# The MLP's token mixing done per pair of heads, and the start, the order of steps and the PSUM banks laid out anew

## The chip, the cores and the metric

The kernel runs on one core of one Trainium2 chip. The time is the device time of one execution in microseconds. Three executions of the kernel before gave 315.58, 315.77 and 318.79, so the median is 315.77 us. The engines are TensorE (PE; PEld is its weight load), VectorE (DVE), ScalarE (ACT), GpSimd (POOL) and SyncE (SP), and each works through its own instructions in their program order.

## The reference

Two stages follow each other. The first is causal attention over 4 batches of 8 heads, 768 positions and 64 dimensions, in which each position sees only its own block of 64 keys and the three blocks with the highest gate scores:

```python
k_rep = k.reshape(B, H, n_blocks, 64, D).mean(axis=3)
gate_scores = einsum('bhsd,bhnd->bhsn', q, k_rep)       # future blocks: -1e9
top_idx = argsort(gate_scores)[..., -3:]                # and the own block
scores = where(chosen block and causal, q @ k.T / sqrt(D), -1e9)
x[b, s, 64 h + d] = softmax(scores) @ v
```

The second is a mixer MLP on `x`, which has 768 positions and 512 channels per batch:

```python
u = x + (relu(x.T @ w_tok1) @ w_tok2).T                 # token mixing, 768 -> 256 -> 768
out = u + relu(u @ w_ch1) @ w_ch2                       # channel mixing, 512 -> 1536 -> 512
```

Token mixing runs over the positions, and every channel stands by itself in it. Channel mixing needs all 512 channels of a position.

## The kernel before

The work goes by pairs of heads (16 pairs, four to a batch) and by heads (32). For each pair, `ktr` transposes K in two halves on TensorE (three fp32 transposes each), copies both heads' parts to `KA` and sums each block's keys on VectorE; `ksd` spreads these sums; `qtr` transposes Q in two halves, and ScalarE copies each half to `QT`; `qcast` makes the 16-bit `QA` of it; `gate` multiplies Q with the block sums (five fp32 matmuls) and finds the third largest score of each row with ten maxima on VectorE; `btr` transposes the resulting bias rows, which go into `QA` as extra contraction rows. Against them, `KA` holds an indicator of the key's block. For each head, `scores` then makes three groups of transposed scores in one of two PSUM tiles of two banks (`sc0`, `sc1`), ScalarE takes their exponential into `E`, `dmask` (GpSimd) zeroes the causal corners, and `avmm` multiplies by V with 21 small matmuls; VectorE divides by the row sum and writes the head's 64 columns of `x`.

The MLP of a batch is a list of steps: `tok1` (two times six matmuls with 512 columns, one column for each channel), `umix` (six times two matmuls with 512 columns, then the residual added on VectorE), `utr` (u transposed, copied by ScalarE), `ch1` (24 steps of four matmuls with 384 columns, with a relu that ScalarE and VectorE take in turn) and `ch2` (six steps of 12 matmuls with 512 columns, a residual on VectorE and a store).

Everything else draws PSUM from a ring of four banks (`bank`). For the last batch `all_banks` adds the four halves of `sc0` and `sc1` at the ring's end.

The order on every engine is set by one list of events: `at(t, f, ...)` gives a step a place t in units of one head, the list is sorted by t, and the functions are called in that order. Head n has its scores at n to n + 0.66 and its `avmm` at n + 1.2; a pair p is prepared from 2p - 3.4 to 2p - 1.2; the MLP of batch b stands evenly, by its matmul columns, between 8(b + 1) + 0.45 and 8(b + 2) + 0.4, so that it lies between the heads of the next batch. The prediction calls such a unit a slot. Loads stand in SyncE's queue, weights in GpSimd's, constants in ScalarE's.

Of the kernel before, what the change touches and what calls it, by code (L numbers as in the profile page):

```python
# [45 lines left out]
def kernel(  # L46
# [65 lines left out]
    h1T = sb([128, 2, DM], F16, "h1T")  # L112
# [19 lines left out]
    def all_banks():  # L132
        ring.extend(t[:, 512 * i:512 * i + 512] for t in sc for i in range(2))
# [13 lines left out]
    own1 = np.where(nidx[None, None, :] == mrow, 0.0, -1.0).astype(np.float16)  # L147
# [75 lines left out]
    def gate(p):  # L223
# [12 lines left out]
        for x in range(2):  # L236
            nc.vector.scalar_tensor_tensor(out=bn[r][:, :, 64 - 64 * x:64 - 64 * x + NB],
                                           in0=ge[r][:, :, NB * x:NB * x + NB],
                                           scalar=1.0, in1=own[:, :, NB * x:NB * x + NB],
                                           op0=ALU.subtract, op1=ALU.max)  # L240

    def btr(p):
# [3 lines left out]
        nc.vector.tensor_copy(out=QA[p % RQ][64:64 + NB, 0, 128:S], in_=t[64:64 + NB, :])  # L246
        nc.vector.tensor_copy(out=QA[p % RQ][0:NB, 1, 128:S], in_=t[0:NB, :])
# [41 lines left out]
    def mlp(b):  # L289
        x, u, ut = xb[b % 2], u16[b % 2], uT[b % 2]  # L290
        th = []

        def tok1(t):
            m = bank()
            for j in range(NJ):
                nc.tensor.matmul(out=m, lhsT=w1[:, j, 128 * t:128 * t + 128], rhs=x[:, j, :],  # L296
                                 start=(j == 0), stop=(j == NJ - 1))
            nc.scalar.activation(out=h1T[:, t, :], in_=m, func=AF.Relu)

        def umix(j):  # L300
            m = bank()
            for t in range(2):
                nc.tensor.matmul(out=m, lhsT=w2[:, t, 128 * j:128 * j + 128], rhs=h1T[:, t, :],
                                 start=(t == 0), stop=(t == 1))
            nc.vector.tensor_tensor(out=u[:, j, :], in0=x[:, j, :], in1=m, op=ALU.add)  # L305

        def utr(j):
            t = bank()[:, 0:256].bitcast(F16)
            for c in range(NCC):
                nc.tensor.transpose(out=t[:, 128 * c:128 * c + 128], in_=u[:, j, 128 * c:128 * c + 128], identity=id16)  # L310
            copy(nc.scalar, ut[:, :, 128 * j:128 * j + 128], t.rearrange("p (c s) -> p c s", s=128))

        def ch1(f, i):
            m = bank()[:, 0:HS]
            for c in range(NCC):
                nc.tensor.matmul(out=m, lhsT=wc1[:, c, 128 * f:128 * f + 128],  # L316
# [102 lines left out]
```

## Time and profile before

| what | us |
|---|---|
| median of three executions | 315.77 |
| the profiled execution | 319.9 |
| its span (first to last instruction) | 318.2 |
| PE busy | 276.8 (87%) |
| DVE busy | 176.6 (55%) |
| ACT busy | 148.3 (47%) |
| POOL busy | 89.2 (28%) |

The profiled execution is 4.1 us above the median and 1.7 us longer than its own span. The busy time of TensorE is the time in which a matmul is under way, and matmuls overlap, so a busy engine is not one at its peak; how far a stretch is from that is read by setting the time of its steps in a dense stretch, one after another, against the time that it took.

### The profile page before, as it was taken

The numbers are of one execution on the slowest core, as the hardware profiler recorded it, in microseconds if no ns is written. First come the engines' busy times: TensorE is split into PE (matmuls) and PEld (weight loads), VectorE is DVE, ScalarE is ACT, GpSimd is POOL, SyncE is SP. The second block draws the span as 40 slices with busy tenths as digits, with TensorE's granted clock in tenths as the row PEclk, the third lists the DMA queues.
The fourth block names the chain that finished last, engine by engine and source line by source line (L and its number), as shares of the span: only waits on it lengthen the run. The fifth ranks groups of instructions, "written<-read, shape, count | busy, mean of one in ns | idle before, by whom it ended". The sixth has DMA issues, their size and how long they took to land.

```text
span 318.2 us, 5946 instructions
## 1 busy us (share of the span) xinstructions
PE 276.8 (87%) x2224; PEld 178.0 (56%) x2224; DVE 176.6 (55%) x533; ACT 148.3 (47%) x233; POOL 89.2 (28%) x167
## 2 busy tenths in 40 slices
PE   2678787698999999889999999889999996778994
PEld 2566575555767665546676656556775453444441
DVE  5966966648575746556757455486755222433221
ACT  1126754657666434556756434466664341532100
POOL 2426756631314141413232333214141120000000
PEclk9999977969999999989999999799999999999999
DMA  8999999995200015896200019800000120000022
GB/s 171 220 218 214 155 215 206 204 230 103 68 21 0 20 50 142 201 222 116 51 2 0 35 66 212 186 0 4 2 0 13 55 98 36 0 1 2 33 81 84
DMA packets 82492, 29.73 MB, mean 93 GB/s; under 512 B 76168, under 2 KB 78880, under 8 KB 82464
## 3 DMA queue, kind: packets, MB, share of 16 engines
q1 hardware_dynamic: 78464, 25.17, 36.5%
q0 software_dynamic: 3232, 3.93, 7.8%
q10 hardware_dynamic: 768, 0.26, 0.4%
q8 instruction: 17, 0.28, 0.4%
q14 instruction: 11, 0.09, 0.1%
HBM read 27.00 MB, written 6.29 MB: 105 GB/s over the span
## 4 chain that ended last, share of the span: by engine, by line
PE 72%; DVE 15%; ACT 3%; DMA 3%; issue 2%; POOL 2%; SPq 0%; DVEq 0%; ACTq 0%; POOLq 0%
PE pm L316 17%; PE pm L327 16%; PE sc L259 9%; PE pm L279 6%; PE pm L227 6%; PE pm L296 4%; PE sc L327 3%; DVE u L305 3%; DVE KA L91 3%; PE pm L202 3%; PE sc L316 2%; PE pm L216 2%; DMA wc<-in_moe_w_ch_dram 2%; DVE ks L205 2%; DMA k<-in_k_dram 1%
## 5 line engine op out<-in xcount | busy, mean ns | idle before, releaser
L262 ACT ACTIVATE E<-sc 128x1024 f16<-128x1024 f32 (+1 forms) x96 | 87.6, 918 | 77.0 <-PE sc L259 72.1
L270 POOL TENSOR_SCALAR_AFFINE_SELECT E<-E 128x256 f16<-128x256 f16 x96 | 39.3, 409 | 158.0 <-ACT E L262 157.0
L316 PE MATMUL pm<-uT,wc 128*128 128x384 f16 x336 | 64.4, 326 | 0.0
L259 PE MATMUL sc<-QA,KA 76*128 76x512 f16 (+7 forms) x256 | 55.7, 325 | 0.0
L327 PE MATMUL pm<-wc,h 128*128 128x512 f16 x240 | 54.9, 379 | 0.0
L316 PEld LDWEIGHTS <-wc 128*128 128x128 f16 x384 | 36.2, 98 | 24.3 <-issue 5.0
L327 PEld LDWEIGHTS <-h 128*128 128x128 f16 x288 | 27.5, 98 | 32.4 <-issue 2.1
L259 PEld LDWEIGHTS <-KA 76*128 76x128 f16 (+1 forms) x256 | 25.4, 107 | 16.9 <-issue 2.2
L322 DVE TENSOR_SCALAR h<-pm 128x384 f16<-128x384 f32 x42 | 23.3, 555 | 18.8 <-PE pm L316 18.5
L331 DVE TENSOR_TENSOR osb<-u,pm 128x512 f32<-128x512 f16 x20 | 13.8, 688 | 35.4 <-PE pm L327 29.9
L279 PE MATMUL pm<-VA,E 128*128 128x65 f16 x672 | 29.2, 200 | 3.4 <-POOL E L270 2.5
L279 PEld LDWEIGHTS <-E 128*128 128x128 f16 x672 | 27.7, 102 | 6.5 <-POOL E L270 4.3
L227 PE MATMUL pm<-ks,QT 128*128 128x24 f32 x160 | 22.4, 283 | 9.7 <-DVE ks L211 9.3
L227 PEld LDWEIGHTS pm<-ks,QT 128*128 128x128 f32 x160 | 22.2, 213 | 12.6 <-ACT E L262 6.8
L205 DVE TENSOR_REDUCE ks<-pm 128x6 f32<-128x384 f32 x32 | 17.4, 544 | 19.5 <-ACT KA L89 19.5
L320 ACT ACTIVATE h<-pm 128x384 f16<-128x384 f32 x42 | 20.5, 489 | 14.5 <-PE pm L316 14.4
L91 POOL CAST QA<-QT 64x768 f16<-64x768 f32 x30 | 24.7, 822 | 9.2 <-ACT QT L217 7.3
L91 DVE CAST KA<-pm 64x384 f16<-64x384 f32 x40 | 22.3, 557 | 2.8 <-PE pm L202 2.1
L202 PE MATMUL pm<-id,k 128*128 128x128 f32 x96 | 19.1, 318 | 5.4 <-DMA k<-in_k_dram 5.4
L217 ACT COPY QT<-pm 128x384 f32<-128x384 f32 x32 | 15.4, 480 | 15.4 <-PE pm L216 15.4
L202 PEld LDWEIGHTS pm<-id,k 128*128 128x128 f32 x96 | 14.0, 171 | 8.7 <-issue 7.3
L285 DVE TENSOR_TENSOR x<-pm,rc 128x384 f16<-128x384 f32 x32 | 17.8, 557 | 1.1
(50 smaller groups left out, 266.6 us busy)
## 6 DMA issues: line engine op xcount, KB each, us to landing
k<-in_k_dram SPq DMA_DIRECT2D x32, 192.0 KB, 4.3
q<-in_q_dram SPq DMA_DIRECT2D x32, 192.0 KB, 4.5
v<-in_v_dram SPq DMA_DIRECT2D x16, 384.0 KB, 5.3
out_dram<-osb SPq DMA_DIRECT2D x24, 256.0 KB, 2.0
wc<-in_moe_w_ch_dram POOLq DMA_DIRECT2D x8, 384.0 KB, 6.7
w<-in_moe_w_tok_dram POOLq DMA_DIRECT2D x2, 384.0 KB, 6.6
id<-id32c ACTq DMA_DIRECT2D x1, 64.0 KB
gbias<-gbiasc ACTq DMA_DIRECT2D x1, 60.0 KB, 3.1
```

The lines of the kernel that those rows point to most:

```text
L91: e.tensor_copy(out=out, in_=in_)
L202: nc.tensor.transpose(out=t[:, 128 * j:128 * j + 128], in_=k32[p % RL][:, 3 * i + j].rearrange("p x d -> p (x d)"), identity=id32)
L205: nc.vector.tensor_reduce(out=ks[p % 2][:, 6 * i:6 * i + 6], in_=t.rearrange("p (n w) -> p n w", w=64), axis=mybir.AxisListType.X, op=ALU.add)
L227: nc.tensor.matmul(out=o[:, j, :], lhsT=QT[r][:, 128 * (j + 1):128 * (j + 2)], rhs=ks2[r].rearrange("p x n -> p (x n)"), start=True, stop= ...
L259: nc.tensor.matmul(out=t[:, at:at + 128 * m], lhsT=KP[0:K, x, 128 * kk:128 * kk + 128], rhs=QP[0:K, x, 128 * q0:128 * (q0 + m)], start=Tru ...
L262: nc.scalar.activation(out=E[n % RE][:, 1024 * g:1024 * g + WIDTH[g]], in_=t[:, 0:WIDTH[g]], func=AF.Exp, scale=scale)
L270: nc.gpsimd.affine_select(out=o, in_=o, pattern=[[0, 2], [1, 128]], compare_op=ALU.is_ge, fill=0.0, base=0, channel_multiplier=-1)
L279: nc.tensor.matmul(out=t[:, jq, :], lhsT=e[:, c:c + 128], rhs=va[:, x, kk, :], start=(kk == 0), stop=(kk == jq))
L316: nc.tensor.matmul(out=m, lhsT=wc1[:, c, 128 * f:128 * f + 128], rhs=ut[:, c, HS * i:HS * i + HS], start=(c == 0), stop=(c == NCC - 1))
L320: nc.scalar.activation(out=o, in_=m, func=AF.Relu)
L322: nc.vector.tensor_scalar(out=o, in0=m, scalar1=0.0, scalar2=None, op0=ALU.max)
L327: nc.tensor.matmul(out=m, lhsT=h2[:, f, 128 * j:128 * j + 128], rhs=wc2[:, f, :], start=(f == 0), stop=(f == NFC - 1))
```

## The change

Token mixing is done per pair of heads. `tok1(p)` takes the pair's 128 channels of `x` (two times six matmuls with 128 columns into one bank, one relu of 256 columns), `umix(p, i)` makes three blocks of positions for these channels in one bank (six matmuls with 128 columns) with one residual of 384 columns, and `utr(p)` transposes the pair's six blocks, with one copy of 768 columns, on VectorE where ScalarE did it before. Only `ch1` and `ch2` are left in the list of the batch; batch b's list starts at 8(b + 1) + `CH[b]` and ends shortly ahead of the next.

At the start, the identity is loaded first, the two gate constants are one tensor (without the copy for the second head), the unused triangle is not loaded, the 16-bit identity is a VectorE cast, the block indicators come by DMA straight into `KA` instead of by six GpSimd copies, and V of pair 0 is loaded behind K and Q of pair 1. K's sums stand ahead of its copies, which ScalarE makes wholly for the first five pairs and by half later. The places of all steps of a pair come from tables by phase (`LEAD`, `MIX`). `all_banks` puts the halves of `sc0` and `sc1` between the four banks, in turn.

```diff
 def all_banks():
-    ring.extend(t[:, 512 * i:512 * i + 512] for t in sc for i in range(2))
+    halves = [t[:, 512 * i:512 * i + 512] for i in range(2) for t in sc]
+    first = [ring[(rn[0] + i) % 4] for i in range(4)]
+    ring[:] = [t for two in zip(first, halves) for t in two]
+    rn[0] = 0
...
+id32 = const(np.eye(128, dtype=np.float32), "id32", nc.scalar)
 load(k32, k, 0, nc.sync)
 load(q32, q, 0, nc.sync)
-id32 = const(...); gbias = const(...); own = const(...); id16 = const(...); m0 = const(...)
-nc.scalar.dma_start(out=ind[0:NB, :], in_=indc)
-nc.scalar.dma_start(out=ind[64:64 + NB, :], in_=indc)
-load(v32, v, 0, nc.sync)
+gown = const(np.ascontiguousarray(np.stack([gb1, own1], axis=1)[:, :, 1:]), "gown", nc.scalar)
+def indicators(r, eng):
+    eng.dma_start(out=KA[r][64:64 + NB, 0, :], in_=indc)
+    eng.dma_start(out=KA[r][0:NB, 1, :], in_=indc)
+nc.vector.memset(KA[0][0:64, 1, :], 0.0)
+indicators(0, nc.scalar)
 load(k32, k, 1, nc.sync)
 load(q32, q, 1, nc.sync)
+load(v32, v, 0, nc.sync)
...
 def ktr(...):
-    copy(e0, KP[0:64, 0, c], t[0:64, :])
     nc.vector.tensor_reduce(out=ks[p % 2][:, 6 * i:6 * i + 6], ...)
-    copy(e1, KP[64:128, 1, c], t[64:128, :])
+    copy(e[0], KP[0:64, 0, c], t[0:64, :])
+    copy(e[1], KP[64:128, 1, c], t[64:128, :])
...
+def tok1(p):
+    b, c = divmod(p, NCC)
+    m = bank()[:, 0:256]
+    for t in range(2):
+        for j in range(NJ):
+            nc.tensor.matmul(out=m[:, 128 * t:128 * t + 128], lhsT=w1[:, j, 128 * t:128 * t + 128],
+                             rhs=xb[b % 2][:, j, 128 * c:128 * c + 128], start=(j == 0), stop=(j == NJ - 1))
+    nc.scalar.activation(out=h1T[p % 2].rearrange("p t c -> p (t c)"), in_=m, func=AF.Relu)
+def umix(p, i):
+    m = bank()[:, 0:HS]
+    for j in range(3):
+        for t in range(2):
+            nc.tensor.matmul(out=m[:, 128 * j:128 * j + 128],
+                             lhsT=w2[:, t, 128 * (3 * i + j):128 * (3 * i + j) + 128],
+                             rhs=h1T[p % 2][:, t, :], start=(t == 0), stop=(t == 1))
+    nc.vector.tensor_tensor(out=u16[b % 2][o], in0=xb[b % 2][o], in1=m.rearrange(...), op=ALU.add)
+def utr(p, e):
+    t = bank()[:, 0:HS].bitcast(F16)
+    for j in range(NJ):
+        nc.tensor.transpose(out=t[:, 128 * j:128 * j + 128], in_=u16[b % 2][:, j, 128 * c:128 * c + 128], identity=id16)
+    copy(e, uT[b % 2][:, c, :], t)
...
+LEAD = [
+    dict(k0=-1.82, k1=-2.59, q0=-1.73, q1=-1.31, ks=-1.1, qc=-0.88, gt=-0.84, vc=-0.16, bt=-0.18),
...
+    dict(k0=-2.32, k1=-1.92, q0=-3.08, q1=-2.09, ks=-1.66, qc=-0.95, gt=-1.43, vc=0.18, bt=-0.52),
+]
+MIX = {2: dict(t1=2.61, u0=3.03, u1=3.03, ut=3.42), 3: dict(t1=2.5, u0=3.05, u1=3.16, ut=3.4)}
+KE = [(A, A), (A, A), (A, A), (V, A)]
+AV, MASK = (1.25, 1.18), 0.23
+CH = [1.69, 1.91, 1.71, 1.9, 0.66]
...
+    at(t0 + o["t1"], tok1, p)
+    at(t0 + o["u0"], umix, p, 0)
+    at(t0 + o["u1"], umix, p, 1)
+    at(t0 + o["ut"], utr, p, V)
...
-    t0, t1 = H * (b + 1) + 0.45, H * (b + 2) + 0.4
+    t0, t1 = H * (b + 1) + CH[b], H * (b + 2) + CH[b + 1] - 0.05
```

Three places of the order are shown, each before and then with the change. In the rows a number behind a name is that of a buffer, and xN counts instructions alike.

The first is VectorE at the start, from the first K transposes (`pm_117`, `pm_118`) to the gate of pair 0 (`gm_87`). Before:

```order
L91 CAST KA_75<-pm_117 64x384
L205 TENSOR_REDUCE ks_83<-pm_117 128x6
...
L91 CAST KA_75<-pm_118 64x384
L205 TENSOR_REDUCE ks_83<-pm_118 128x6
...
L211 COPY ks_0_85<-ks_83 64x12 x2
L91 CAST QA_72<-QT_81 64x768 x2
L229 TENSOR_TENSOR gm_87<-pm_117,gbias 128x120
```

With the change:

```order
L178 CAST id_138<-id_122 128x128
L207 TENSOR_REDUCE ks_83<-pm_118 128x6
L207 TENSOR_REDUCE ks_83<-pm_119 128x6
L214 COPY ks_0_85<-ks_83 64x12 x2
L91 CAST QA_72<-QT_81 64x768 x2
L235 TENSOR_TENSOR gm_87<-pm_118,gown 128x120
```

The four casts into `KA` have left VectorE's queue; they stand in ScalarE's, ahead of the copies to `QT`.

The second is TensorE behind the gate of pair 0, up to the first scores (`sc`). Before, K's and Q's transposes of pair 1 and its gate (`ks_1_86`) stand ahead of them:

```order
L227 MATMUL pm_117<-ks_0_85,QT_81 128x24 x5
L202 MATMUL pm_118<-id_125,k_1_67 128x128 x3
L245 LDWEIGHTS bn_93
...
L202 MATMUL pm_120<-id_125,k_1_67 128x128 x3
L216 MATMUL pm_117<-id_125,q_1_64 128x128 x3
L216 MATMUL pm_118<-id_125,q_1_64 128x128 x3
L227 MATMUL pm_119<-ks_1_86,QT_82 128x24 x5
L259 LDWEIGHTS KA_75
L259 MATMUL sc_115<-QA_72,KA_75 128x512
```

With the change:

```order
L231 MATMUL pm_118<-ks_0_85,QT_81 128x24 x5
L219 MATMUL pm_119<-id_122,q_1_64 128x128 x3
L251 LDWEIGHTS bn_93
...
L219 MATMUL pm_121<-id_122,q_1_64 128x128 x3
L265 LDWEIGHTS KA_75
L265 MATMUL sc_116<-QA_72,KA_75 128x512
```

K's transposes and the gate of pair 1 now stand between and behind the first scores; only Q's transposes are left ahead of them.

The third is ScalarE in batch 0, from the first exponential of one pair of heads to that of the next. Before:

```order
L262 ACTIVATE E_97<-sc_115 128x1024
L262 ACTIVATE E_97<-sc_116 128x1024
L262 ACTIVATE E_97<-sc_115 128x640
L262 ACTIVATE E_95<-sc_116 128x1024
L217 COPY QT_82<-pm_119 128x384
L262 ACTIVATE E_95<-sc_115 128x1024
L217 COPY QT_82<-pm_117 128x384
L262 ACTIVATE E_95<-sc_116 128x640
```

With the change:

```order
L268 ACTIVATE E_97<-sc_116 128x1024
L89 CAST KA_77<-pm_120 64x384 x2
L221 COPY QT_81<-pm_121 128x384
L89 CAST KA_77<-pm_118 64x384 x2
L268 ACTIVATE E_97<-sc_117 128x1024
L302 ACTIVATE h1T_102<-pm_121 128x256
L268 ACTIVATE E_97<-sc_116 128x640
L268 ACTIVATE E_95<-sc_117 128x1024
L268 ACTIVATE E_95<-sc_116 128x1024
L268 ACTIVATE E_95<-sc_117 128x640
L221 COPY QT_82<-pm_119 128x384
```

The four casts of K and the relu of token mixing have come into the queue, between the first and the third exponential of the pair.

## Rows read from the trace of the kernel before

**Rows 1.** Stages: from:to us, length, then busy us of engines, PEclk, DMA share.

```profile
21.60:66.50 44.90, 35.81 (x347) 27.64 (x347) 32.31 (x122) 26.44 (x37) 27.52 (x49) 0.88 1.13 201
66.50:134.50 68.00, 65.22 (x556) 42.14 (x556) 41.29 (x128) 38.49 (x61) 20.51 (x39) 0.98 0.38 86
134.50:202.70 68.20, 65.34 (x557) 42.31 (x557) 41.29 (x128) 37.47 (x60) 19.45 (x37) 0.98 0.42 94
202.70:265.10 62.40, 59.35 (x501) 36.71 (x501) 31.78 (x86) 32.09 (x50) 14.12 (x29) 0.98 0.13 36
265.10:277.00 11.90, 7.82 (x49) 3.68 (x49) 4.10 (x6) 4.12 (x7) 0.00 (x0) 1.00 0.06 22
277.00:297.00 20.00, 16.53 (x98) 9.35 (x96) 6.13 (x11) 6.47 (x13) 0.00 (x0) 1.00 0.01 1
297.00:318.20 21.20, 15.90 (x73) 6.84 (x70) 4.68 (x7) 0.00 (x0) 0.00 (x0) 1.00 0.20 74
```

**Rows 2.** Chain that ended last, 66 to 110 us: start us, us, what.

```profile
69.87 1.30 PE pm L296 x6
...
76.11 0.22 PE pm L310 x4
...
80.25 0.65 PE pm L316 x4
80.90 1.03 PE pm L227 x10
...
82.58 0.44 PE sc L259 x3
...
83.67 0.66 PE pm L279 x21
...
86.72 0.33 PE pm L202 x3
...
88.62 0.28 PE pm L245 x5
...
106.80 2.59 PE pm L327 x12
```

**Rows 3.** Timeline of the start: start us, us, engine, line, operation, [idle before <-releaser].

```profile
9.08 0.48 ACT L217 COPY QT<-pm 128x384 f32<-128x384 f32 x1 [0.16 <-PE pm L216]
...
10.66 2.30 PE L227 MATMUL pm<-ks,QT 128*128 128x24 f32 x10 [1.62 <-DVE ks L211]
...
15.05 0.69 PE L245 MATMUL pm<-id,bn 128*128 128x128 f16 x5 [1.38 <-DVE bn L237]
...
19.42 2.30 PE L227 MATMUL pm<-ks,QT 128*128 128x24 f32 x10 [1.75 <-DVE ks L211]
...
22.61 1.02 ACT L262 ACTIVATE E<-sc 128x1024 f16<-128x1024 f32 x1 [4.43 <-PE sc L259]
```

**Rows 4.** Timeline of TensorE in batch 0, one gate.

```profile
50.97 1.27 PE L227 MATMUL pm<-ks,QT 128*128 128x24 f32 x10 [1.95 <-DVE ks L211]
```

**Rows 5.** Groups by line and shape: busy us, mean ns, idle before.

```profile
L262 ACT ACTIVATE E<-sc 128x1024 f16<-128x1024 f32 x64 | 65.4, 1024 | 70.7 <-PE sc L259 70.3
...
L262 ACT ACTIVATE E<-sc 128x640 f16<-128x640 f32 x32 | 22.6, 706 | 6.3 <-POOL QA L91 3.6 <-PE sc L259 1.8
...
L217 ACT COPY QT<-pm 128x384 f32<-128x384 f32 x32 | 15.4, 480 | 15.4 <-PE pm L216 15.4
...
L89 ACT CAST KA<-pm 64x384 f16<-64x384 f32 x24 | 11.2, 468 | 6.0 <-PE pm L202 5.8
```

**Rows 6.** Waits from 264 us to the end: us in total, times, longest.

```profile
PE sc L316 <- ACT h L320: 3.5, 6, 0.6
```

**Rows 7.** The last piece of the chain, columns as in rows 2.

```profile
314.50 0.69 DVE osb L331
```

**Rows 8.** Waits of the whole span, columns as in rows 6.

```profile
PE pm L296 <- DVE x L285: 2.6, 2, 1.3
...
PE pm L310 <- DVE u L305: 5.1, 7, 1.2
```

More of the change, by code (lines that the diff above doesn't have):

```diff
@@ L286, in avmm @@
                                 in1=r.broadcast_to([128, NJ, 64]), op=ALU.mult)
[L289 to L294, printed above, removed]
-            for j in range(NJ):
[L296 to L301, printed above, removed]
-            for t in range(2):
[L303 to L316, printed above, removed]
-                                 rhs=ut[:, c, HS * i:HS * i + HS], start=(c == 0), stop=(c == NCC - 1))
-            o = h2[:, f, HS * i:HS * i + HS]
-            if f % 2 == 0:
-                nc.scalar.activation(out=o, in_=m, func=AF.Relu)
-            else:
-                nc.vector.tensor_scalar(out=o, in0=m, scalar1=0.0, scalar2=None, op0=ALU.max)
-        def ch2(j):
-            m = bank()
-            for f in range(NFC):
-                nc.tensor.matmul(out=m, lhsT=h2[:, f, 128 * j:128 * j + 128], rhs=wc2[:, f, :],
-                                 start=(f == 0), stop=(f == NFC - 1))
-            o = osb[osn[0] % 3]
-            osn[0] += 1
-            nc.vector.tensor_tensor(out=o, in0=u[:, j, :], in1=m, op=ALU.add)
-            nc.sync.dma_start(out=out[b, 128 * j:128 * j + 128, :], in_=o)
-        th += [(3072, lambda t=t: tok1(t)) for t in range(2)]
-        for j in range(NJ + 1):
-            if j < NJ:
-                th.append((1024, lambda j=j: umix(j)))
-            if j >= 1:
-                th.append((512, lambda j=j: utr(j - 1)))
-        th += [(1536, lambda f=f, i=i: ch1(f, i)) for i in range(2) for f in range(NFC)]
-        th += [(6144, lambda j=j: ch2(j)) for j in range(NJ)]
-        return th
@@ new lines, in utr, with ch1 @@
+    def utr(p, e):
+        b, c = divmod(p, NCC)
+        t = bank()[:, 0:HS].bitcast(F16)
+        for j in range(NJ):
+            nc.tensor.transpose(out=t[:, 128 * j:128 * j + 128], in_=u16[b % 2][:, j, 128 * c:128 * c + 128],
+                                identity=id16)
+        copy(e, uT[b % 2][:, c, :], t)
+    def ch1(b, f, i):
+        m = bank()[:, 0:HS]
+        for c in range(NCC):
+            nc.tensor.matmul(out=m, lhsT=wc1[:, c, 128 * f:128 * f + 128],
+                             rhs=uT[b % 2][:, c, HS * i:HS * i + HS], start=(c == 0), stop=(c == NCC - 1))
+        o = h2[:, f, HS * i:HS * i + HS]
+        if f % 2 == 0:
+            nc.scalar.activation(out=o, in_=m, func=AF.Relu)
+        else:
+            nc.vector.tensor_scalar(out=o, in0=m, scalar1=0.0, scalar2=None, op0=ALU.max)
@@ new lines, in ch2 @@
+    def ch2(b, j):
+        m = bank()
+        for f in range(NFC):
+            nc.tensor.matmul(out=m, lhsT=h2[:, f, 128 * j:128 * j + 128], rhs=wc2[:, f, :],
+                             start=(f == 0), stop=(f == NFC - 1))
+        o = osb[osn[0] % 3]
+        osn[0] += 1
+        nc.vector.tensor_tensor(out=o, in0=u16[b % 2][:, j, :], in1=m, op=ALU.add)
+        nc.sync.dma_start(out=out[b, 128 * j:128 * j + 128, :], in_=o)
+    A, V, G = nc.scalar, nc.vector, nc.gpsimd
+    LEAD = [
+        dict(k0=-1.82, k1=-2.59, q0=-1.73, q1=-1.31, ks=-1.1, qc=-0.88, gt=-0.84, vc=-0.16, bt=-0.18),
+        dict(k0=-1.95, k1=-1.61, q0=-2.79, q1=-2.08, ks=-1.36, qc=-1.44, gt=-1.26, vc=-0.16, bt=-0.34),
+        dict(k0=-1.76, k1=-1.87, q0=-2.04, q1=-1.83, ks=-1.75, qc=-1.49, gt=-1.6, vc=-0.89, bt=-0.84),
+        dict(k0=-2.32, k1=-1.92, q0=-3.08, q1=-2.09, ks=-1.66, qc=-0.95, gt=-1.43, vc=0.18, bt=-0.52),
+    ]
@@ L374 @@
             at(n + 0.33 * g, scores, n, g)
[L375 to L376 removed]
+            at(n + 0.33 * g + MASK, dmask, n, g)
+        at(n + AV[0 if n < H else 1], avmm, n)
+    at(2 * NP - 0.1, all_banks)
     for b in range(B):
[L378 to L382 removed]
+        th = [(1536, ch1, b, f, i) for i in range(2) for f in range(NFC)] + [(6144, ch2, b, j) for j in range(NJ)]
+        total = sum(c for c, *_ in th)
+        t0, t1 = H * (b + 1) + CH[b], H * (b + 2) + CH[b + 1] - 0.05
         done = 0
[L384 to L385 removed]
+        for c, f, *a in th:
+            at(t0 + (t1 - t0) * done / total, f, *a)
             done += c
```

99 lines of the change are left out of this document (48 added, 51 removed).

## The prediction

> **What bounds the kernel now.** I read the stages first [rows 1], then the chain of waits in the dense part for the price of each step [rows 2], then the start [rows 3], one cycle of batch 0 [rows 4], and the end [rows 6, 7]. From 66.5 us to 265 us TensorE is under way for 95% of each stage, and the chain there is nearly one matmul step after another. So I take the time of a step in that chain as its price at the full clock, add up the whole kernel in these prices, and call what is left of the span the loss. The change can only win out of the loss, or change the work.
>
> Prices in us: three K transposes 0.33, and three for Q, the same instruction on another tensor, as much; a gate 1.03; the five bias transposes 0.28; a score group of 1024 columns 0.44, so one of 640 columns 0.28; an `avmm` 0.66; four `ch1` matmuls 0.65; twelve `ch2` matmuls 2.59; six `tok1` matmuls of 512 columns 1.30; four transposes of u 0.22 [rows 2].
>
> A pair of heads: 0.66 + 0.66 + 1.03 + 0.28 + 2 x (0.44 + 0.44 + 0.28) + 2 x 0.66 = 6.27, of which 2.63 is its preparation; 16 pairs are 100.3. Channel mixing of a batch: 24 x 0.65 + 6 x 2.59 = 31.1; four are 124.6. Token mixing of a batch: 2 x 1.30, as much for the twelve `umix` matmuls of equal width, and 6 x 0.22, so 6.5; four are 26.1. The work is 251.0, and the loss 318.2 - 251.0 = 67.2.
>
> Where it lies, by stage. Up to 66.5 us, slot 8.45, TensorE has done 31.0 of work (five preparations and a sixth without its bias transposes 15.5; scores of eight heads and two groups 10.2; eight `avmm` 5.3): a loss of 35.5. Batches 1 and 2 [rows 1] hold 6.27 x 4 + 6.5 + 31.1 = 62.7 of work in 68.0 and 68.2: 5.3 and 5.5. The stage of 62.4 holds what is left, 57.0: 5.4. After attention, 53.1 for 37.6: 15.5.
>
> **The work added.** `tok1` and `umix` turn 24 matmuls of 512 columns per batch into 96 of 128, each with its own weight load. The nearest row is the u transposes, 128 columns with a load each, at 0.22 / 4 = 0.055 us; `avmm`, 65 columns with a load each, runs at 0.66 / 21 = 0.031 [rows 2], so a load does not set the pace down to there. I take 0.055: a pair's token mixing is 30 x 0.055 = 1.65, in all 26.4 against 26.1. The work becomes 251.3. The bounds are 0.053 (a quarter of the 512-column matmul, 2.59 / 48) and 0.076, the mean time of a weight load in batch 1 (42.14 us over 556, [rows 1]), should nothing of it hide.
>
> The Trainium skill, "TensorE: Matmul & The Clock Gate", section "Back-to-back issue gap", speaks against this part: it gives 81 ns a matmul for a sustained stream of load and matmul at 128 columns, and 131 ns at 512. By it the 384 matmuls would cost 384 x 0.026 = 10.0 us more than in my sum, which would end at 294. The trace disagrees with it at both widths, with 55 ns and 216 ns, and I go by the rows.
>
> **The start, to the first scores.** Now the gate of pair 0 starts at 10.66, 1.1 us after the second half of QT is there (9.08 + 0.48), since VectorE is still making K's casts and sums; and the first scores wait for a second gate, which starts at 19.42, so that the first exponential is at 22.61 [rows 3]. With the casts on ScalarE, ahead of the QT copies but in time that it waited for Q, the sums are spread before QT is copied, so the gate starts at 9.7. It takes the same 2.3 us (low clock: it takes 1.03 at the full one). The bias transposes come 15.05 - 12.96 = 2.1 later and take 0.7, the copies of the bias some 0.7 more: scores at 15.5, the first exponential at 16.4, 6.2 earlier. Fewer constants, the direct indicators and the identity cast save nothing more on this path, which runs through K, Q and the gate; their engines have room there. V of pair 0, behind K and Q of pair 1, is wanted only by the first `avmm`, after that exponential.
>
> **Batch 0.** Its 44.9 us hold 8.45 slots, so 10.6 us for each pair, against 6.27 of work. The row shows why: every gate waits some 1.95 us for VectorE's sums [rows 4], and such a wait is followed by a low clock (mean 0.88 in the stage, [rows 1]). Now token mixing joins, so TensorE has 7.9 per pair. ScalarE has 2 x (2 x 1.024 + 0.706) + 2 x 0.48 + 4 x 0.468 [rows 5] and a relu of 256 columns, under 0.48, say 0.38: 8.7. VectorE's 7.6 (32.31 x 10.6 / 44.9) lose four casts and gain two adds and a copy: about 7. So ScalarE sets the floor. Following its queue from the first exponential of a pair: QT is whole after 1.02 + 2 x 0.47 + 0.48 = 2.4; the gate (1.03), `tok1` (0.66) and the third score group (0.28) then run while ScalarE makes two casts and the second exponential (to 4.4), the relu and the third (to 5.5) and the fourth (to 6.5). The fifth wants scores that stand behind the next `avmm`, which wants the third exponential masked: about 7.3. So it waits 0.7, and the cycle is 8.7 + 0.7 + 0.1 = 9.5. TensorE waits for QT about 0.6 a cycle in place of 1.95, and the clock should hold. Bounds: 8.7, and 10.6 + 1.65 = 12.2, if every wait stays and token mixing is added to it.
>
> Channel mixing now starts at slot 9.69: 15.5 + 4.85 x 9.5, and 1.0 for pair 5's first steps that stand beside pair 4's: 62.6 us. Work done by then: preparations 16.4, ten heads' scores 11.6, nine `avmm` 5.9, four token mixings 6.6: 40.5. The loss is 22.1.
>
> **Batches 1 to 3.** What goes is token mixing as one block: `tok1` waiting for the last head's x, transposes waiting for the adds [rows 8], and the low clock behind it (0.98, [rows 1]). In the new order a pair's `avmm`, `tok1`, `umix` and `utr` stand 0.32, 0.55 and 0.24 slots apart, 2.5, 4.3 and 1.9 us, with `ch1` or `ch2` between. What is late next is VectorE, strictly in order: 41.3 of 68 now, about 44 of 65 with u's copies from ScalarE; adds, a u copy, a relu and a gate's ten maxima come close together, and each holds one of four banks. I take a loss of 2.5 a batch, half of today's; the bounds are 0.7 and today's 5.4. Three: 7.5.
>
> **The end.** The last pair's steps stand between three `ch2` steps of batch 2; exposed are about a relu (0.6) and a u copy (0.9). In `ch1`, 20.0 us for 15.6 of work, TensorE waits six times for a relu where both halves of one `sc` tile stand next to each other in the ring [rows 6]; with the halves four places apart I leave 0.5 for this and for `ch2`. From the last residual to the end 3.7 stay [rows 7]. Together 5.7, against 15.5.
>
> **The sum.** 251.3 + 22.1 + 7.5 + 5.7 = 286.6, that is 31.6 less than the span, so 288.3 for the profiled execution's 319.9. The median is 4.1 below that one; taking 31.6 from 315.77 gives 284.
>
> **The rivals.** (a) *Batch 0 keeps its waits*: a cycle of 12.2 adds 4.85 x 2.7 = 13, so 297; halfway it is 291. For it: ScalarE is loaded to nine tenths, and all queues are in order. Against: the reduce stands ahead of the casts. 0.16. (b) *VectorE becomes the bound beside channel mixing*: 5.4 a batch stay, 8.7 more, 293. For it: more small steps per bank. Against: TensorE stays at 95% in stages where VectorE is at 60%. 0.11. (c) *Weight loads do not hide behind 128 columns*: 0.076 each, 384 x 0.021 = 8 more, 292; the transposes speak against it. 0.04. The skill's rule above is this case. (d) *The ring still waits for its neighbours*: 4.4 stay, 288. 0.05. (e) *All queues mesh*: a cycle of 8.7 and 0.7 a batch give 284 - 3.9 - 5.4 = 275. 0.06. (f) *Slower*: the token chain stalls TensorE in every pair, not once in a batch: for x, for the relu, for the adds. Waits of this kind last up to 1.3 and 1.2 us today [rows 8]; three of them are 2.5 to 3.7 a pair, and 16 pairs lose 40 to 59, so 324 at the least. It decides from (31.6 + 3.2) / 16 = 2.2 us a pair on. Against it stand the distances in slots above, and other matmuls between. 0.03.
>
> **The numbers.** The forecast, 284 with its own range of 278 to 290, has 0.55. A measurement of this kernel can tell about 1% from no change. All cases but (f) are over 1% faster; I leave 0.02 for a mixture that ends near zero: faster 0.95, same 0.02, slower 0.03. From 275, case (e), to 297, case (a) at its bound, no more than 2 in 10 is left out.
>
> **What would show it.** In the profile after: the first exponential near 16.4 us; a first `ch1` near 63; gates of batch 0 9.5 us apart with waits under 1 us and a clock near 1.0; matmuls of `tok1` 0.055 apart; about 65 us from one batch's `ch1` to the next; the last `ch1` in about 16 us and hardly a wait on `sc`. I would be wrong if batch 0 stretched past 12 us a pair, or if TensorE's waits for VectorE grew in the dense stages.

## The result, and the profile after

The change takes 281.27 us (median of four executions, 280.13 to 285.02) against 317.28 for the kernel before in the same comparison: a ratio of 0.884, 95% interval 0.874 to 0.895. The forecast of 284 was 2.7 us high, and the range of 275 to 297 held it. Ratios here and below compare means, and leave out executions over 1.5% longer than the fastest of their kernel (here the one of 285.02). The profiled execution took 281.06, its span 279.0, which is 39.2 less than the 318.2 of the profile before; by the medians the kernel is 36.0 shorter.

The stages of the kernel after, cut at the first exponential, at the first `ch1` of each batch and at the end ([rows 1] were cut a little ahead of the first exponential, and at the first `tok1` of each batch). Columns: stretch in us, its length, busy us and instruction count of each engine, granted clock, DMA share, GB/s:

```profile
0.00:15.80 15.80, 7.17 (x38) 5.61 (x39) 8.00 (x33) 5.59 (x11) 3.35 (x11) 0.88 1.06 194
15.80:61.60 45.80, 43.28 (x522) 35.86 (x521) 33.33 (x131) 37.93 (x60) 28.23 (x51) 0.89 1.18 219
61.60:125.20 63.60, 63.51 (x634) 45.20 (x632) 41.45 (x131) 37.34 (x61) 19.61 (x37) 1.00 0.45 104
125.20:188.50 63.30, 63.16 (x627) 44.46 (x625) 41.26 (x130) 37.46 (x60) 19.22 (x36) 1.00 0.46 102
188.50:243.50 55.00, 54.42 (x534) 36.73 (x532) 30.78 (x86) 27.90 (x46) 13.67 (x27) 1.00 0.10 32
243.50:279.00 35.50, 31.44 (x171) 16.30 (x168) 11.82 (x20) 5.89 (x12) 0.00 (x0) 0.99 0.14 53
```

Stage by stage, with the experiments that are told below (spans of the profiled executions, in us; the three batches run from one batch's first `ch1` to the next):

| kernel | to first exp | exp to first `ch1` | batches | last `ch1` to end | span |
|---|---|---|---|---|---|
| before | 22.6 | 57.5 | 68.1, 68.2, 60.4 | 41.4 | 318.2 |
| after | 15.8 | 45.8 | 63.6, 63.3, 55.0 | 35.6 | 279.0 |
| e1 pairs only, old ring | 22.4 | 54.5 | 66.6, 63.6, 56.4 | 41.9 | 305.4 |
| e5 pairs, new ring | 22.3 | 55.5 | 66.6, 63.6, 54.5 | 35.6 | 298.1 |
| e2 order only | 16.7 | 57.1 | 68.3, 66.6, 59.4 | 35.0 | 303.1 |
| e6 order, useless matmuls | 16.4 | 53.9 | 66.6, 67.0, 59.0 | 35.0 | 297.9 |
| e3 old ring | 16.4 | 47.8 | 63.6, 63.3, 56.8 | 41.9 | 289.9 |
| e10 K's casts on VectorE | 16.7 | 59.1 | 63.6, 63.4, 54.9 | 35.6 | 293.3 |

So the 39.2 are 6.8 at the start, 11.7 in batch 0, 14.8 in the batches and 5.8 at the end (the rest is rounding). In the first two batches TensorE is under way for 63.51 of 63.60 us and 63.16 of 63.30, where [rows 1] had about 96%.

At the start, the timeline of the kernel after (start us, length, engine, line, operation, tiles; in brackets the idle time before it and what ended it) answers to [rows 3]:

```profile
9.40 1.29 PE L231 MATMUL pm<-ks,QT 128*128 128x24 f32 x10 [0.82 <-ACT QT L221]
13.46 0.69 PE L251 MATMUL pm<-id,bn 128*128 128x128 f16 x5 [2.26 <-DVE bn L243]
15.78 1.02 ACT L268 ACTIVATE E<-sc 128x1024 f16<-128x1024 f32 x1
```

The gate now waits for QT and no longer for the sums, and the scores need one gate instead of two. (e10 below, with K's casts on VectorE again, has its first exponential at 16.7, so the casts are worth 0.9 of the 6.8.) In batch 0 the gates answer to [rows 4]:

```profile
28.38 1.26 PE L231 MATMUL pm<-ks,QT 128*128 128x24 f32 x10
37.26 1.35 PE L231 MATMUL pm<-ks,QT 128*128 128x24 f32 x10
46.20 1.35 PE L231 MATMUL pm<-ks,QT 128*128 128x24 f32 x10
55.78 1.26 PE L231 MATMUL pm<-ks,QT 128*128 128x24 f32 x10 [1.09 <-ACT E L268]
```

They are 8.9, 8.9 and 9.6 us apart (that of pair 1 is at 19.08, that of pair 2 the first shown), and the wait of 1.95 us for `ks` is gone. The granted clock is not high in the whole of batch 0. It is 0.50 in every slice of 4 us from 12 to 24 us, 0.81 in the next, and 1.00 in each from 28 to 72:

```profile
20.00:24.00 4.00, 4.00 (x34) 3.22 (x35) 2.18 (x16) 1.61 (x2) 1.01 (x3) 0.50 1.24 238
28.00:32.00 4.00, 3.90 (x47) 3.26 (x46) 3.09 (x19) 3.94 (x8) 2.84 (x5) 1.00 1.07 199
```

In the dense part the chain of waits (start, us, what) shows the pair's token mixing as three short links, and this answers to [rows 2, 8]:

```profile
116.63 0.67 PE pm L300 x12
...
119.43 0.67 PE pm L309 x12
...
123.78 0.34 PE pm L320 x6
```

Between them stand other matmul steps, without a gap. TensorE's whole list of waits for VectorE or ScalarE inside the MLP is two short ones at the end (waiter, releaser, total us, times, longest); [rows 8] had 2.6 and 5.1 us, and [rows 6] 3.5 us on `sc`:

```profile
PE sc L309 <- ACT h1T L302: 0.5, 1, 0.5
PE sc L329 <- DVE uT L91: 0.4, 1, 0.4
```

### The profile page after: what moved, and what is told of

Read it like the earlier page. It is cut to its first block, busy times and chain, and to the rows that moved or that the text cites. A ratio compares the mean times of both kernels' runs of the same rounds, so it can differ in the third digit from the quotient of the medians.

```text
span 279.0 us, 6475 instructions
## 1 busy us (share of the span) xinstructions
PE 263.0 (94%) x2512; PEld 184.2 (66%) x2512; DVE 166.6 (60%) x528; ACT 152.1 (55%) x247; POOL 84.1 (30%) x161
## 4 chain that ended last, share of the span: by engine, by line
PE 86%; DVE 5%; ACT 5%; DMA 1%; issue 1%; SPq 0%; DVEq 0%; ACTq 0%
PE pm L329 19%; PE pm L340 18%; PE sc L265 12%; PE pm L285 7%; PE pm L231 6%; PE sc L340 5%; PE pm L204 4%; PE pm L309 4%; PE pm L300 3%; PE pm L219 3%; PE sc L329 3%; ACT KA L89 2%; PE pm L251 2%; PE pm L320 2%; ACT E L268 1%; DMA k<-in_k_dram 1%
## 5 line engine op out<-in xcount | busy, mean ns | idle before, releaser
L276 POOL TENSOR_SCALAR_AFFINE_SELECT E<-E 128x256 f16<-128x256 f16 x96 | 39.2, 408 | 136.8 <-ACT E L268 136.0
L329 PE MATMUL pm<-uT,wc 128*128 128x384 f16 x336 | 66.7, 326 | 0.2
L340 PE MATMUL pm<-wc,h 128*128 128x512 f16 x228 | 52.3, 379 | 0.0
L335 DVE TENSOR_SCALAR h<-pm 128x384 f16<-128x384 f32 x48 | 26.6, 554 | 17.3 <-PE pm L329 16.0
L344 DVE TENSOR_TENSOR osb<-u,pm 128x512 f32<-128x512 f16 x19 | 13.1, 688 | 31.1 <-PE pm L340 28.5
L285 PE MATMUL pm<-VA,E 128*128 128x65 f16 x672 | 27.2, 195 | 0.0
L285 PEld LDWEIGHTS <-E 128*128 128x128 f16 x672 | 25.6, 99 | 1.4
L89 ACT CAST KA<-pm 64x384 f16<-64x384 f32 x42 | 19.9, 473 | 9.6 <-DVE KA L91 4.1
L231 PEld LDWEIGHTS pm<-ks,QT 128*128 128x128 f32 x160 | 20.4, 200 | 4.9 <-ACT E L268 1.3
L204 PE MATMUL pm<-id,k 128*128 128x128 f32 x96 | 17.1, 293 | 5.4 <-DMA k<-in_k_dram 5.4
L333 ACT ACTIVATE h<-pm 128x384 f16<-128x384 f32 x36 | 17.7, 491 | 3.1 <-PE pm L329 2.9
L221 ACT COPY QT<-pm 128x384 f32<-128x384 f32 x32 | 15.2, 477 | 6.8 <-PE pm L219 5.9
L313 DVE TENSOR_TENSOR u<-x,pm 128x384 f16<-128x384 f16 x31 | 16.4, 549 | 4.0 <-PE pm L309 3.5
```

Of the source, the lines that this page charges most:

```text
L89: e.copy(out=out, in_=in_)
L231: nc.tensor.matmul(out=o[:, j, :], lhsT=QT[r][:, 128 * (j + 1):128 * (j + 2)], rhs=ks2[r].rearrange("p x n -> p (x n)"), start=True, stop= ...
L276: nc.gpsimd.affine_select(out=o, in_=o, pattern=[[0, 2], [1, 128]], compare_op=ALU.is_ge, fill=0.0, base=0, channel_multiplier=-1)
L285: nc.tensor.matmul(out=t[:, jq, :], lhsT=e[:, c:c + 128], rhs=va[:, x, kk, :], start=(kk == 0), stop=(kk == jq))
L335: nc.vector.tensor_scalar(out=o, in0=m, scalar1=0.0, scalar2=None, op0=ALU.max)
L340: nc.tensor.matmul(out=m, lhsT=h2[:, f, 128 * j:128 * j + 128], rhs=wc2[:, f, :], start=(f == 0), stop=(f == NFC - 1))
```

## Experiments

The theory after the result has three parts. In batch 0, token mixing per pair fills time in which TensorE waited, and keeps its clock up from 28 us on; K's casts on ScalarE take the wait for `ks` away. In the batches, spreading the token chain removes the block's waits. At the end, the order of the ring's halves removes the waits on `sc`. Rivals: one part alone makes the gain; batch 0 is quick because the start leaves TensorE warm; the distances in the token chain are not needed.

**e1 and e5, pairs alone.** The kernel before with the per-pair `tok1`, `umix`, `utr` at the change's places, and the change's times for `ch1`, `ch2` and the weights. The start, the constants, `ktr` and the tables for preparation stay.

```diff
 # kernel before, both runs:
+def tok1(p): ...   def umix(p, i): ...   def utr(p, e): ...
+MIX = {...}; CH = [1.69, 1.91, 1.71, 1.9, 0.66]
 # e5 only, in all_banks():
-    ring.extend(t[:, 512 * i:512 * i + 512] for t in sc for i in range(2))
+    halves = ...; ring[:] = [t for two in zip(first, halves) for t in two]
```

> The kernel before with token mixing per pair alone (its weights earlier, the list of channel mixing as in the change, the ring in the new order); constants, first loads, K's casts and the leads of 3.4 to 1.2 slots are those of before. Theory (losses lie by place, start and batch 0 are cured by the order, batches and end by token mixing per pair): first exponential at 22.6 us as before, batch 0 at 10.6 to 12.2 us a pair because the waits of each gate stay, channel mixing starting at 73 to 81 us, from there the same 63 to 64 us a batch and the same end of about 40 us as in the change: span 290 to 298. Rival (the two parts only work together, and the long leads make TensorE wait for the token chain in the batches): over 302. Rival (token mixing per pair is the whole gain): under 284.

> The first experiment (token mixing per pair alone) once more, this time really with the ring in the new order; there it was still the old one. Theory: only the end changes, from 41.9 us after the first channel mixing of the last batch to 34 to 36, so a span of 297 to 300 against 305.4. Rival (the 11 us that the first experiment was longer behind batch 0 come from its long leads in the batches): 303 or more.

The first of them ran with the old ring, contrary to what its expectation says of it, so e5 repeats it as meant; both are told, since together they price the ring. e1 took 307.96 (ratio 0.971, 0.962 to 0.980), e5 300.2 (0.949, 0.943 to 0.955). e1's span of 305.4 missed the expected 290 to 298, and e5's 298.1 came as expected. The batches get 12.0 us of the 14.8 (e5 against before; e1, with the old ring, gets 10.1). Batch 0 gets only 2.0 to 3.0. The last stage is 41.9 against 35.6, so 6.3 us for the ring there.

**e2, order alone.** The change with the MLP of before: token mixing by batch, u copied by ScalarE.

```diff
-at(t0 + o["t1"], tok1, p) ... at(t0 + o["ut"], utr, p, V)
-th = [(1536, ch1, ...)] + [(6144, ch2, ...)]
+th = mlp(b)          # tok1, umix, utr, ch1, ch2 of the batch, as before
+t0, t1 = H * (b + 1) + 0.45, H * (b + 2) + 0.4
```

> The change with token mixing by batch as in the kernel before (its list from slot 8(b+1) + 0.45, its u copy on ScalarE); start, leads, K's casts, the ring are the change's. Theory: first exponential at about 15.8 us, batch 0 at 8.5 to 9 us a pair, so token mixing of batch 0 starts at 51 to 54 us where it was 66.5; batches keep about 68 us and the end some 49 us (4 less, by the ring): span 298 to 303. Rival (the order is nearly the whole gain): under 290. Rival (the order is only good with work of token mixing in its gaps): over 308.

It took 302.09 (0.955, 0.946 to 0.964), so the total came out as expected, but not the place. The start gains 5.9, the batches 2.4 and the end 6.4; batch 0 gains 0.4, where I had looked for it to become quicker. From the first exponential to `tok1` it takes 45.8 us, so 10.8 a pair. The two orders of work thus gave 2.0 and 0.4 in batch 0 alone, and 11.7 together. The stretch from 32 to 48 us of this kernel shows a low clock (the columns are those of the stages above):

```profile
32.00:40.00 8.00, 5.90 (x58) 4.47 (x58) 4.64 (x13) 4.32 (x6) 4.29 (x9) 0.79 1.14 221
40.00:48.00 8.00, 5.86 (x66) 4.37 (x63) 5.88 (x23) 4.94 (x9) 4.74 (x8) 0.78 1.04 216
```

**e6, order with useless matmuls.** To tell a fuller TensorE from the token chain itself: e2 with 30 matmuls of 128 columns per pair, of the identity by itself, at the places where the change has token mixing in batch 0. Nobody reads them.

```diff
 # e2 with
+def filler(n):
+    m = bank()[:, 0:128]
+    for _ in range(n):
+        nc.tensor.matmul(out=m, lhsT=id16, rhs=id16, start=True, stop=True)
+if p < H // 2:
+    for name, cnt in (("t1", 12), ("u0", 6), ("u1", 6), ("ut", 6)):
+        at(t0 + MIX[2][name], filler, cnt)
```

> The second experiment (the order alone, span 303.1, channel mixing from 73.8 us, 10 to 12 us a pair in batch 0) with useless matmuls added for pairs 0 to 3: 12, 6, 6 and 6 of 128 columns at the very places where the change has tok1, umix and utr, into a bank that nobody reads; their result is not used. They are 4 x 1.68 = 6.7 us of work more. Theory (in the new order the token mixing fills gaps of TensorE, and without it the clock falls and batch 0 crawls): batch 0 gets quicker with more work, 9 to 9.5 us a pair, channel mixing from 66 to 69 us, span 295 to 299. Rival (the gaps and the clock do not matter, the queues of the other engines set the pace): channel mixing from 73 to 78 us, span 303 to 308.

It took 299.51 (0.947, 0.942 to 0.952), although 120 matmuls of no use, some 120 x 0.056 = 6.7 us, were added. That is 2.6 us less than e2 by the medians, each of the four executions under the shortest of e2's; the two ran on different chips, and the intervals of their ratios overlap. The profiles differ by 5.2 us, but e2's is that of its longest execution (305.1), and 1.7 of the 5.2 lie in the batch behind batch 0, where the two programs are alike. 3.5 lie ahead of the first `ch1`. The same two stretches now, and the one behind them:

```profile
32.00:40.00 8.00, 7.57 (x99) 6.19 (x96) 5.32 (x24) 6.89 (x12) 4.96 (x11) 1.00 1.12 211
40.00:48.00 8.00, 7.64 (x108) 6.38 (x105) 4.84 (x17) 6.69 (x11) 5.64 (x10) 1.00 1.08 205
48.00:56.00 8.00, 7.39 (x83) 6.09 (x82) 4.54 (x18) 4.54 (x7) 4.01 (x9) 0.79 1.11 190
```

The clock is 1.00 instead of 0.79 and 0.78. It falls to 0.79 in the third stretch, where TensorE waits 0.6 us for Q's load, useless matmuls or not. TensorE's wait for the gate's bias (`bn`) falls from 6.4 us in four waits to one of 1.6. From the first exponential to `tok1` it is 41.1 us, 9.7 a pair instead of 10.8; the first `ch1`, at 70.3, came a little later than expected. So in batch 0 the added matmuls cost less than nothing: they stand in time in which TensorE waited, and the work around them runs at the higher clock. e6 still has token mixing of batch 0 as a block, 12.8 us from `tok1` at 57.5 to the first `ch1`, with attention steps and the last 30 useless matmuls in it. In the change token mixing itself stands at these places and the block is gone. I take that for the rest of the way from 53.9 to 45.8 in this stage; no run shows it by itself.

**e10 and e9, K's casts back on VectorE.** e4 and e10 are the same kernel. e4's executions have a median of 298.33, but its profile is that of the longest, with a span of 323.6 and a granted clock of 0.84, so the traces of e10 are read.

```diff
-KE = [(A, A), (A, A), (A, A), (V, A)]
+KE = [(V, V), (V, V), (V, V), (V, A)]
 # e4 and e10 also, in ktr(); e9 leaves ktr() as changed:
+copy(e[0], KP[0:64, 0, c], t[0:64, :])
 nc.vector.tensor_reduce(...)
-copy(e[0], KP[0:64, 0, c], t[0:64, :])
```

> The change with K's casts of the first five pairs back on VectorE, the first cast of each half ahead of the sum. ScalarE's load in batch 0 falls from 8.7 to 6.8 us a pair, VectorE's rises from about 7 to 9.3. Theory (the sums behind the casts made every gate wait): gates 10 to 11 us apart instead of 9.0, each with a wait for VectorE of 1 us or more and the clock falling behind it: 5 to 9 us longer than the change. Rival (ScalarE's load is the floor of batch 0): 0 to 4 us shorter.

> The fourth experiment once more, for a trace at the usual clock (its first one was taken at a granted clock of 0.84). Theory: every gate of batch 0 waits 1.8 to 2.1 us for VectorE's sums, 10.5 to 11.5 us apart, the rest as in the change: 12 to 15 us longer than the change. Rival (the length came from the clock alone): within 4 us of the change.

> The change with K's casts of the first five pairs on VectorE, but behind the sum of their half, as in the change. Theory (what made the gates wait in the fourth experiment is the cast that stands in front of the sums in the same queue): one cast still stands in front of the second half's sum, so the gates of batch 0 are 9.5 to 10.5 us apart with waits for VectorE under 1.5 us: 2 to 7 us longer than the change. Rival (VectorE's load alone): as slow as the fourth experiment, 12 us or more longer than the change. Rival (ScalarE is the floor): shorter than the change.

e10 took 295.35 (0.931, 0.924 to 0.939), e9 297.62 (0.939, 0.932 to 0.946); the two spans are equal at 293.3, 14.3 longer than the change's, nearly all of it in batch 0 (59.1 for 45.8). VectorE ahead of a gate of e10:

```profile
51.66 0.55 DVE L91 CAST KA<-pm 64x384 f16<-64x384 f32 x1 [1.20 <-PE pm L204]
52.13 0.54 DVE L208 TENSOR_REDUCE ks<-pm 128x6 f32<-128x384 f32 x1
...
54.90 0.78 DVE L214 COPY ks<-ks 64x12 f32<-64x12 f32 x2
55.73 2.33 PE L231 MATMUL pm<-ks,QT 128*128 128x24 f32 x10 [2.36 <-DVE ks L214]
```

and of the change:

```profile
44.45 1.21 DVE L207 TENSOR_REDUCE ks<-pm 128x6 f32<-128x384 f32 x2 [0.53 <-PE pm L204]
45.69 0.35 DVE L214 COPY ks<-ks 64x12 f32<-64x12 f32 x2
```

From the start of the first reduction to the end of the copies it is 1.6 us in the change and 3.6 in e10. TensorE waits 2.36 us for it, and the gate behind that wait takes 2.33 us in place of 1.35. Sums ahead of casts (e9) bring nothing, where I had expected e9 to be only 2 to 7 us longer than the change, because `ksd`'s copies stand behind all four casts in either order. What counts is the engine of the casts, not their place within `ktr`; casts on VectorE behind `ksd`'s copies were not tried.

**e3, the old ring.** The change with the one line of `all_banks` of before.

```diff
-halves = ...; first = ...; ring[:] = [t for two in zip(first, halves) for t in two]; rn[0] = 0
+ring.extend(t[:, 512 * i:512 * i + 512] for t in sc for i in range(2))
```

> The change with the four halves of sc0 and sc1 put at the ring's end, as before, so that both halves of a tile stand next to each other. Theory (a matmul into one half waits for the reader of the other): the last channel mixing's first part takes 20 us instead of 15.7, and its second some 1.5 more: 4 to 6 us longer than the change. Rival (the ring's order is of no account since eight banks are enough): within 1 us of the change.

It took 292.24 (0.920, 0.909 to 0.930). Its profile is 10.9 longer than the change's, over the expected 4 to 6. The last stage has 6.3 of it, as between e1 and e5, and the chain there shows how:

```profile
250.03 0.66 PE sc L326 x4
...
250.71 0.50 ACT h L330
...
251.25 0.82 PE sc L326 x4
...
252.17 0.57 DVE h L332
```

The second half of an `sc` tile is written only when the relu has read the first half, while with the halves four places apart [rows 6] is gone. Besides the relu, `ch2` waits for the residual of the other half, twice 0.8 us, so the list of waits of this stage names 5.1 us for the ring. Another 1.8 us lie in the stage ahead, where the ring already differs. There the last pair's `tok1` and second `umix` wait for readers of the other half:

```profile
242.22 0.83 PE L297 MATMUL sc<-x,w 128*128 128x128 f16 x12 [0.84 <-DVE osb L341]
244.72 0.49 PE L306 MATMUL sc<-h1T,w 128*128 128x128 f16 x6 [0.70 <-DVE u L310]
```

e1 has the same two waits, and e5 and the change have neither. The remaining 2.6 lie before the first `ch1`, where the two programs are alike, so they are not the ring. 0.6 of them come with the first gate (2.33 us for 1.29) and 1.6 behind pair 5's: after the same wait of 1.09 us ahead of that gate, the granted clock from 56 to 60 us is 0.72 in e3 and 1.00 in the change.

**e7, TensorE kept warm.** 9 and 7 matmuls of zeros, 512 columns each, ahead of the first K transposes and between the first gate and the scores.

```diff
+at(-5.0, warm, 9)
+at(-0.5, warm, 7)
```

> The change with useless matmuls of zeros at the start, which nobody reads: nine of 512 columns ahead of K's first transposes, while TensorE waits for K, and seven between the gate of pair 0 and its bias transposes. In the change the granted clock is 0.5 from about 12 to 25 us. Theory (from 13.5 to 25 us TensorE is the bound at that clock): at the full clock the stretch is 3 to 5 us shorter, channel mixing from 57 to 59 us instead of 61.6, span 274.5 to 276.5. Rival (the useless matmuls only stand in front of the transposes, or ScalarE is the bound there): 279 to 282.

283.28 (0.889, 0.883 to 0.895), span 278.9: nothing, as the rival said. The clock did rise, to 0.73 from 12 to 16 us and 1.00 from 16 to 20, where the change has 0.50, and the first `ch1` is at 61.5 for 61.6. So the start does not leave TensorE warm in the change, and batch 0 is quick all the same. Pair 2's gate came 0.6 us sooner (27.82 for 28.38), and pair 5's gate, at 55.69 for 55.78, gave it back.

**e8 and e11, the distances of the token chain.** e8 puts a pair's steps directly behind each other, e11 halves the distances.

```diff
-MIX = {2: dict(t1=2.61, u0=3.03, u1=3.03, ut=3.42), 3: dict(t1=2.5, u0=3.05, u1=3.16, ut=3.4)}
+MIX = {2: dict(t1=2.26, u0=2.27, u1=2.28, ut=2.29), 3: dict(t1=2.19, u0=2.2, u1=2.21, ut=2.22)}    # e8
+MIX = {2: dict(t1=2.43, u0=2.64, u1=2.64, ut=2.84), 3: dict(t1=2.34, u0=2.62, u1=2.67, ut=2.79)}    # e11
```

> The change with a pair's token mixing placed in one go right behind the pair's second avmm: tok1, umix, umix, utr with nothing between them. Theory (rival f of the prediction: the distances hide the waits for x, for the relu and for the adds): TensorE waits 2.5 to 3.7 us in every pair, 40 to 59 us in all, span 319 to 338, slower than the kernel before. Rival (other slack takes it up, the distances matter little): under 294.

> The change with the distances between avmm, tok1, umix and utr of a pair halved. Between a pair's second avmm and its tok1 there is then one score group of 0.43 us, between umix and utr nothing or one ch1 step. From the closed chain (eighth experiment: waits of 1.1 for x, 0.5 for the relu, 0.35 for the adds in every pair, and 52 us in all): about 0.7 of the first and 0.35 of the last are left, some 1 us a pair. Theory (what a wait costs is its uncovered part, and no more while the clock holds): 8 to 18 us longer than the change. Rival (half the distance covers all): within 3 us. Rival (the clock falls behind any wait in every pair): over 25 us.

e8 took 333.29 (1.054, 1.049 to 1.060), span 331.4: 52.4 more than the change and slower than before. It is rival (f), and its total lies in the 40 to 59 of the prediction. One pair of it, on TensorE:

```profile
106.81 0.84 PE L300 MATMUL pm<-x,w 128*128 128x128 f16 x12 [1.21 <-DVE x L291]
108.13 0.83 PE L309 MATMUL pm<-h1T,w 128*128 128x128 f16 x12 [0.47 <-ACT h1T L302]
109.33 0.80 PE L320 MATMUL pm<-id,u 128*128 128x128 f16 x6 [0.37 <-DVE u L313]
```

These are 2.05 us of waiting in a pair, less than the 2.5 to 3.7 of the prediction. In all it is 16.3 us for x, 7.6 for the relu and 5.4 for u, 29.3 of the 52.4. The waits for the gate's bias are 8.6 us where the change has 2.3, and TensorE is under way for 278.2 us instead of 263.0, 15.2 more for the same matmuls. 22.2 of the 52.4 lie in batch 0, whose clock is 0.83. So the total came out as priced, but in part by luck: the waits that the price was made of are little more than half of it.

e11 took 321.19 (1.016, 1.009 to 1.023), span 318.6: 39.6 more, where I had expected 8 to 18. It is not a smaller e8. Its waits for x are 4.0 us in all, but VectorE is late with u, 18.1 us in 15 waits. VectorE around one of them:

```profile
112.62 0.82 DVE L238 MAX8 m<-gm 128x8 f32<-128x12 f32 x10
113.80 1.13 DVE L243 SCALAR_TENSOR_TENSOR bn<-ge,gown 128x60 f16<-128x60 f32 x2
114.85 1.01 DVE L313 TENSOR_TENSOR u<-x,pm 128x384 f16<-128x384 f16 x2
```

and TensorE:

```profile
108.42 2.75 PE L340 MATMUL pm<-wc,h 128*128 128x512 f16 x12
...
115.45 0.97 PE L320 MATMUL pm<-id,u 128*128 128x128 f16 x6 [2.30 <-DVE u L313]
117.70 4.53 PE L340 MATMUL pm<-wc,h 128*128 128x512 f16 x12
```

At this distance the residuals stand behind a gate's ten maxima and its bias in VectorE's queue, so that TensorE waits 2.30 us; in 11 of the 16 pairs eight or ten maxima stand between `umix` and the second residual, in the change never more than four. The twelve `ch2` matmuls behind this wait take 4.53 us, where twelve of the same ahead of it took 2.75, so this wait is paid nearly twice. Over the whole span it is less: of the 39.6, TensorE is idle for 26.2 more (42.2 for 16.0) and under way for 13.4 more (276.4 for 263.0). The rival of a clock that falls behind any wait, over 25 us, thus fits the total, but at most a third of it can be its cause.

**e12, pair 5's gate.** The one wait of over 1 us left in the change beside the start is at pair 5's gate (55.78, above). Its sums and gate earlier, and its casts on the engines of the later pairs:

```diff
+if p == H // 2 + 1:
+    o = dict(o, ks=-1.8, gt=-1.38)
-ke, be = KE[ph], BE[ph]
+ke, be = KE[2 if p == H // 2 + 1 else ph], BE[ph]
```

> The change with two steps of pair 5 moved: its K casts all on ScalarE and its sums spread ahead of the division of head 7, so that its gate does not wait, and tok1 of pair 3 ahead of that gate. In the change TensorE waits 1.1 us there, the only wait over 0.7 us between 20 us and the end of attention. Theory: channel mixing starts 1 to 1.5 us earlier, at about 60.3 us, and the span is 277.5 to 278.5; of the median hardly to be told. Rival (the wait moves to another step of that pair): as the change.

282.1 (0.891, 0.886 to 0.896), span 280.1. The wait went, and one of 0.6 us of pair 3's `tok1`, now ahead of that gate, for x took its place. The expected span of 277.5 to 278.5 was missed; it is the same as the change. No experiment gave a version that beats it.

## Why the prediction was right, step by step

**The work.** Twelve `tok1` matmuls of 128 columns take 0.67 us, as twelve `umix` do: 0.056 each, against the 0.055 that I took. With 384 of them the work is 251.7. Rival (c), loads that do not hide, is out. So is the rule of the Trainium skill that it goes with ("TensorE: Matmul & The Clock Gate", "Back-to-back issue gap", 81 ns at 128 columns): this trace disagrees with it, at 56 ns.

**The start.** First exponential at 15.8, forecast 16.4; the path was as described. The gate took 1.29 and not 2.3 us. With a gate of 2.33 us, e3 and e12 come to 16.39 and 16.41, so the forecast had this path right, and the 0.6 is the quicker gate of the one execution. What makes it quick was not found: e7's gate takes 2.33 us at a granted clock of 0.50, but e3's and e12's take as long where the profile gives 1.00.

**Batch 0.** First `ch1` at 61.6 for 62.6, a loss of 21.1 for 22.1, and 8.9 to 9.6 us a pair for 9.5. The wait for QT of 0.6 us a cycle, for which ScalarE was to be the floor, is not in the list of waits; the only one for QT is 0.8 us at the first gate. Rival (a) fell. But the reason that I gave against it was wrong: it said that the reduction stands ahead of the casts, and e9 shows that this order is worth nothing; moving the casts to ScalarE is what takes 14.3 us out. The claim that "the clock should hold" was right from 28 us on only: the mean of the stage is 0.89, hardly over the 0.88 of before, and the sign of a clock near 1.0 did not come. By e7 the low stretch up to there costs nothing. e2 and e6 show that token mixing's own matmuls are part of what holds the clock behind it, which the prediction did not see: it counted them as work that makes the cycle longer.

**Batches 1 to 3.** This is the step that failed in size. I took a loss of 2.5 a batch, half of that before, 7.5 in all. The three take 181.9 us; the work that falls into them is 251.7 - 40.5 up to the first `ch1` - 31.1 after the last = 180.1, so that the loss is 1.8, 0.6 each and just under the lower bound of 0.7. VectorE, which I named as next to be late, is not late at these distances; e11 shows that it is at half of them. So the distances in slots were the right argument, and halving the loss was too cautious a reading of it. Rival (b) fell with it.

**The end.** 35.5 less 31.1 of work is a loss of 4.4 for the forecast 5.7: some 0.6 around the last u copy, a wait of 0.4 in the list, and 3.7 from the last matmul to the end. The wait of 0.5 us for the last relu lies just ahead of this stage. Nothing is left on `sc` for a relu or a residual of `ch1` and `ch2`, so rival (d) fell too; e1 with e5, and e3, put the ring's order at 6.3 us in this stage, more than the 3.5 of waits in [rows 6], which leave out the 1.6 that `ch2` waits for the residual.

**The sum.** The span was forecast at 286.6 and came to 279.0. The 7.6 are 1.0 up to the first `ch1`, 5.7 in the batches and 1.3 at the end, less 0.4 of work. In the median only 2.7 are seen, since the profile before was of an execution 4.1 above its median; that the forecast looks so close there is luck. With hardly a wait left, this is close to rival (e), all queues mesh, in the batches, and not in batch 0. Rival (f) is shown to exist, at e8's distances.

Open: what makes the first gate quick or slow, why the clock fell behind a wait of 1.09 us in e3 and not in the change (in e6 it fell behind one of 0.6), and what the new places of K's and Q's steps (`LEAD`) and the fewer constants bring by themselves; no run takes them apart.

## What to carry to other kernels

Price a chain of small steps by the distances between them, against what stands ahead of each releaser in its own queue: at full distance the three batches lost 1.8 us in all, and at half of it the kernel is 39.6 longer, 18.1 of it in waits for adds, most of which had come to stand behind a gate's maxima. Where TensorE waits again and again (2.30 us in e11, 2.36 in e10), count the slower matmuls behind the wait along with the wait, and look for real work to put there before shortening the rest. Two edits that do little alone (2.0 and 0.4 us in batch 0) can be worth 11.7 together, so price the stage with both in it.

## What the runs showed that was not expected

Useless matmuls made a kernel faster: 120 of them, 6.7 us of work, took 2.6 us off the median and brought the first `ch1` 3.5 us forward (e6 against e2). Useless matmuls at the start, where nothing but the path through K, Q and the gate counts, were worth nothing (e7). After a wait of 2.30 us the next twelve matmuls took 4.53 us instead of 2.75 (e11), so what follows a wait can cost almost as much as the wait. And two halves of one PSUM tile that follow each other in the ring cost 6.3 us in the 24 `ch1` and six `ch2` steps at the end, and 1.8 ahead of them, where the list of waits names 5.1 and 1.5.
